# Loading the first batch through the casting DMA queue, in a fused cross-attention and maxout kernel

## The chip, the cores and the metric

The kernel runs on one core of one Trainium2 chip. A core has a matrix engine (TensorE, PE in the profile), a vector engine (VectorE, DVE), an activation engine (ScalarE, ACT), a general engine (GpSimd, POOL) and a synchronization engine (SyncE, SP). Each runs its own instruction stream in order and waits for the others by semaphores. SP and POOL also issue the DMA transfers here: SP's go by a hardware queue (q1 in the profile) and move bytes as they are; POOL's go by a software queue (q0) and can cast float32 to bfloat16 on the way. Matrix results land in PSUM, everything else lives in SBUF.

The metric is the device time of one execution in microseconds. The kernel before took 166.1 us, the median of five runs from 165.62 to 167.12.

## The reference

There are 8 batches with 8 heads each. For each head there is x (512 rows of 64) and a state (32 rows of 64).

```
scores = x @ state.T / 8          # 512 x 32
a      = softmax(scores)          # over the 32 states
xread  = a @ state                # 512 x 64
a2     = softmax(state @ x.T / 8) # over the 512 rows of x
sread  = a2 @ x                   # 32 x 64
rows   = concat(xread, sread)     # per batch 544 rows of 8 * 64 = 512
h      = max(rows @ w1, rows @ w2, rows @ w3)   # 768 wide
out    = h @ w_out                # 4352 x 512
```

Inputs and output are float32. The kernel computes in bfloat16 with float32 sums.

## The kernel before, in words

**Layout.** Batch b's x lies in `x_sb[b]`: partition p holds 4 consecutive rows of each of the 8 heads, so 8 runs of 256 numbers, and behind them 64 columns of ones (L82), which the state read (`sread`, L217) uses to get the denominator of its softmax from the same matmul. The states of two batches are loaded together (`st_f[k]`, `load_st`, L57), cast to bfloat16 twice side by side (`states_cast`, L126), transposed by PE and spread into `bds[k]` (`states`, L132 and L135), a block-diagonal layout in which a pair of heads can be served by one matmul. The rest of `bds[k]` must be zero, hence the memsets of `bds` (L104, L105, L322).

**The work per batch.** `x_transpose` puts x on its side in two halves, even heads (g = 0) and odd heads (g = 1): eight PE transposes into PSUM and a copy out (L151, L154). `scores` multiplies with the states and takes the exponential on ACT (L172, L177). `softmax` sums and divides (L184 to L187). `a_transpose` turns the weights (L198, L199). Instead of computing xread and multiplying it with W, `g_cols` (L240) multiplies the states with 384 columns of the three W at once (128 of each, a slice m of six) and ACT or DVE copies the result G out of PSUM (L246). `maxout` (L261) multiplies the transposed weights with G, three matmul pairs for the three W, and ACT (L265) and DVE (L268, L269) take the maximum. `ffn_out` (L286, L293) multiplies with w_out and stores by DMA (L297, L302).

**Weights.** W comes in three chunks of columns, of 1, 2 and 3 slices. Chunk 0, the first slice, is loaded as float32 by SP in three parts, one for each W (`w0_f`, L102), and cast by ACT (L332). Chunks 1 and 2 are loaded and cast by POOL's queue (`load_w`, L91), three transfers each.

**Order.** The order of all instructions is written out by hand: an engine executes its instructions in the order of the program text, and the tile framework adds only the semaphores. A PSUM or SBUF buffer of a rotating tag is taken when the one who had it is done: tag "pw" has four PSUM buffers, which the transposes, the maxout matmuls and the output matmuls take in turn; tag "two" has two larger ones. `keep_busy(n)` issues n matmuls on zeros whose result nobody reads (L117).

The first batch comes in like this. SP loads the first two batches' states, then x of batch 0 as float32 in two halves (`x0_f`, L75), then W's first slice in three parts. POOL builds the identity matrix, writes the ones of all eight batches and the zeros of `bds[1]`, and then issues the load of batch 1 and six loads of W. PE runs five filler matmuls, transposes the states, runs three more, and transposes batch 0 as DVE (even heads, L319) and ACT (odd heads, L320) have cast it. After the scores of batch 0 PE runs four fillers and goes on with the transposes of batch 1.

POOL's transfers take their completion semaphores from a group of eight in turn. A transfer that comes to a semaphore a second time is issued only when the earlier transfer on it has landed.

## Time and profile before

| | |
|---|---|
| five runs | 165.62, 166.04, 166.1, 166.91, 167.12 us |
| profiled execution | 166.1 us, of which the instructions span 164.3 us |
| busy share of the span | PE 93%, ACT 62%, DVE 58%, POOL 25% |
| 0 to 4 us | PE busy 2.81, ACT 1.49, DVE 1.18, POOL 3.40 us |
| 8 to 12 us | PE busy 3.64, ACT 2.23, DVE 2.56, POOL 1.34 us |
| 32 to 36 us | PE busy 3.59, ACT 2.78, DVE 3.62, POOL 0 us |
| bytes moved by DMA | 21.59 MB; 14.42 by POOL's queue, 6.95 by SP's |

The profile is of one execution. A group of instructions is named by the line of the kernel, the engine, and what it writes and reads. In the timeline and in the chain, the first number is the start in us and the second the duration; "x8" counts instructions; what stands in brackets is how long the engine was idle before the group and who released it. "PEld" is PE's loading of the stationary operand, which runs beside its matmuls.

### The profile page before, as it was taken

The numbers are of one execution on the slowest core, as the hardware profiler recorded it, in microseconds if no ns is written. First come the engines' busy times: TensorE is split into PE (matmuls) and PEld (weight loads), VectorE is DVE, ScalarE is ACT, GpSimd is POOL, SyncE is SP. The second block draws the span as 40 slices with busy tenths as digits, with TensorE's granted clock in tenths as the row PEclk, the third lists the DMA queues.
The fourth block names the chain that finished last, engine by engine and source line by source line (L and its number), as shares of the span: only waits on it lengthen the run. The fifth ranks groups of instructions, "written<-read, shape, count | busy, mean of one in ns | idle before, by whom it ended". The sixth has DMA issues, their size and how long they took to land.

```text
span 164.3 us, 3574 instructions
## 1 busy us (share of the span) xinstructions
PE 152.4 (93%) x1432; PEld 72.7 (44%) x1448; DVE 94.7 (58%) x160; ACT 101.7 (62%) x163; POOL 41.8 (25%) x61
## 2 busy tenths in 40 slices
PE   7699799998999999999999999999999999999990
PEld 2356243543345444444344444343444456665440
DVE  2573987879518653674548454855485555585001
ACT  3568458676896778854786688648764853333440
POOL 8933640105150601081016101410141010100140
PEclk9999999999999999999999999999999999999999
DMA  4999999900029999449991988460306030030374
GB/s 119 326 204 198 204 199 250 135 6 2 0 107 152 128 255 195 92 81 138 277 217 73 129 190 104 165 192 14 128 0 192 14 128 0 0 132 0 128 221 162
DMA packets 31824, 21.59 MB, mean 131 GB/s; under 512 B 15648, under 2 KB 29344, under 8 KB 31808
## 3 DMA queue, kind: packets, MB, share of 16 engines
q0 software_dynamic: 13520, 14.42, 42.4%
q1 hardware_dynamic: 18288, 6.95, 20.9%
q8 instruction: 11, 0.18, 0.4%
q14 instruction: 5, 0.04, 0.1%
HBM read 15.20 MB, written 8.91 MB: 147 GB/s over the span
## 4 chain that ended last, share of the span: by engine, by line
PE 63%; DVE 13%; ACT 12%; issue 4%; DMA 4%; POOL 1%; SPq 0%; DVEq 0%; ACTq 0%
PE pw L261 32%; PE po L286 20%; DVE t L268 4%; ACT G L246 4%; DVE ht L269 4%; PE pg L240 4%; DVE den L184 4%; DMA x0f<-in_x_dram 3%; ACT e L177 3%; ACT t L265 2%; PE ps L172 2%; PE psr L217 2%; DMA out_dram<-osb 1%; PE pxt L151 1%; PE idle L117 1%
## 5 line engine op out<-in xcount | busy, mean ns | idle before, releaser
L261 PE MATMUL pw<-aT,G 128*128 128x512 bf16 x288 | 71.3, 379 | 3.4 <-ACT G L246 2.1
L268 DVE TENSOR_TENSOR t<-t,pw 128x512 bf16<-128x512 bf16 (+1 forms) x54 | 35.0, 649 | 40.5 <-ACT t L265 38.5
L286 PE MATMUL po<-wout,ht 128*128 128x512 bf16 x188 | 47.9, 380 | 0.8
L261 PEld LDWEIGHTS <-G 128*128 128x128 bf16 x288 | 26.7, 98 | 36.1 <-issue 4.5
L246 ACT CAST G<-pg 128x768 bf16<-128x768 f32 x47 | 35.8, 805 | 8.3 <-PE pg L240 8.0
L265 ACT CAST t<-pw 128x512 bf16<-128x512 f32 (+1 forms) x54 | 30.5, 565 | 13.9 <-PE pw L261 12.4
L269 DVE TENSOR_TENSOR ht<-t,pw 128x512 bf16<-128x512 bf16 (+1 forms) x54 | 35.5, 658 | 5.6
L293 ACT COPY osb<-po 128x512 f32<-128x512 f32 x33 | 19.4, 587 | 21.2 <-PE po L286 20.7
L286 PEld LDWEIGHTS <-ht 128*128 128x128 bf16 x204 | 18.4, 98 | 23.6 <-issue 4.7
L302 POOL DMA_DIRECT2D out_dram<-osb x14 | 7.8, 559 | 70.2 <-ACT osb L293 70.2
L187 POOL TENSOR_TENSOR a<-e,rden 128x1024 bf16<-128x1024 bf16 (+1 forms) x8 | 14.4, 1800 | 36.4 <-DVE rden L186 29.8
L240 PE MATMUL pg<-w,bd 64*32 64x384 bf16 x384 | 13.2, 328 | 0.2 <-DVE G L246 0.2
L184 DVE TENSOR_REDUCE den<-e 128x32 f32<-128x1024 bf16 (+1 forms) x9 | 9.9, 1101 | 4.4 <-ACT e L177 4.4
L177 ACT ACTIVATE e<-ps 128x1024 bf16<-128x1024 f32 x7 | 7.2, 1025 | 4.6 <-PE ps L172 4.6
L261 PE MATMUL pw<-ats,w 128*128 128x256 bf16 x72 | 8.8, 273 | 0.0
L240 PEld LDWEIGHTS <-bd 64*32 64x32 bf16 x384 | 3.7, 89 | 11.0 <-issue 10.8
L261 PEld LDWEIGHTS <-w 128*128 128x128 bf16 x72 | 7.0, 98 | 2.1
L151 PE MATMUL pxt<-ident,x 128*128 128x128 bf16 x64 | 6.1, 260 | 1.8 <-ACT x L320 0.8
L135 ACT COPY bd<-pt 64x512 bf16<-64x512 bf16 x8 | 4.6, 580 | 4.1 <-PE pt L132 4.0
L151 PEld LDWEIGHTS <-x 128*128 128x128 bf16 x64 | 5.1, 119 | 4.1 <-DVE x L319 1.6
L117 PE MATMUL idle<-zero 128*128 128x512 bf16 x12 | 5.7, 630 | 1.2 <-DVE zero L78 1.2
L69 POOL DMA_DIRECT2D x<-in_x_dram x7 | 6.7, 956 | 0.0
(44 smaller groups left out, 67.1 us busy)
## 6 DMA issues: line engine op xcount, KB each, us to landing
out_dram<-osb POOLq DMA_DIRECT2D x14, 512.0 KB, 3.5
x<-in_x_dram POOLq DMA_DIRECT2D x7, 512.0 KB, 9.1
w<-in_moe_w_dram POOLq DMA_DIRECT2D x3, 384.0 KB, 13.6
x0f<-in_x_dram SPq DMA_DIRECT2D x2, 512.0 KB, 4.6
w0f<-in_moe_w_dram SPq DMA_DIRECT2D x3, 256.0 KB, 5.8
w<-in_moe_w_dram POOLq DMA_DIRECT2D x3, 256.0 KB, 10.0
wout<-in_moe_w_out_dram POOLq DMA_DIRECT2D x1, 768.0 KB, 16.1
out_dram<-osb SPq DMA_DIRECT2D x1, 512.0 KB, 2.7
```

Of the source, the lines that this page charges most:

```text
L151: nc.tensor.transpose(p[:, s, jj, :], xv[b][:, 2 * s + g, 2 * jj:2 * jj + 2, :].rearrange("p j d -> p (j d)"), ident)
L177: nc.scalar.activation(out=e[b][:, :, g0:g1], in_=p, func=AF.Exp, scale=scale)
L184: nc.vector.reduce_sum(out=den, in_=e[b][:, :, g0:g1], axis=AX.X)
L187: mul(out=a[b][:, :, g0:g1].rearrange("p j g s n -> p j (g s) n"), in0=e[b][:, :, g0:g1].rearrange("p j g s n -> p j (g s) n"), in1=rden.r ...
L240: nc.tensor.matmul(p[32 * s:32 * s + 32, g, 0:384].rearrange("p (i f) -> p i f", i=3), bd(b, 2 * s + g)[64 * g:64 * g + 64, g, :], w[64 * ...
L246: copy(out=G[b][:, :, m * 384:(m + 1) * 384], in_=p[:, :, 0:384])
L261: nc.tensor.matmul(p[:, 0:n], lhs(i, k), rhs(k), start=(k == 0), stop=(k == nk - 1))
L265: nc.scalar.copy(out=t0[:, 0:n], in_=pw[0][:, 0:n])
L268: nc.vector.tensor_max(t1[:, 0:n], t0[:, 0:n], pw[1][:, 0:n])
L269: nc.vector.tensor_max(ht[b][:, m, :], t1[:, 0:n], pw[2][:, 0:n])
L286: nc.tensor.matmul(p, ht[b][:, m, j * 128:(j + 1) * 128], wout_sb[:, m, :], start=(m == 0), stop=(m == NM - 1))
L293: nc.scalar.copy(out=o[:, j, :], in_=p)
```

## The change

Four things change in the prologue, and one copy later moves to another engine.

1. x of batch 0 is no longer loaded as float32 by SP and cast by DVE and ACT. POOL's queue loads and casts it, in two halves, as the first transfers that POOL issues.
2. W's first slice: parts 1 and 2 stay with SP and are cast by ACT; part 3 is loaded and cast by POOL's queue, behind x of batch 1.
3. The ones of all batches and the zeros of `bds[1]` are written by DVE, behind its cast of the first states, where it wrote `bds[2]` and `bds[3]`; these are no longer behind DVE's cast of x.
4. The second run of fillers has four matmuls instead of three.
5. The second pair of states is spread into `bds[1]` by DVE instead of ACT.

```diff
-    x0_f = [data.tile([128, HS, J * D], F32, name=f"x0f{g}") for g in range(2)]
-    for g in range(2):
-        nc.sync.dma_start(
-            out=x0_f[g], in_=x[0].rearrange("(s g) (p j) d -> g p s (j d)", g=2, j=J)[g])
     zero = const.tile([128, 512], BF16, name="zero")
     nc.vector.memset(zero, 0.0)
     ident = const.tile([128, 128], BF16, name="ident")
     make_identity(nc, ident)
-    for b in range(B):
-        nc.gpsimd.memset(x_sb[b][:, XW:XW + D], 1.0)
+    for g in range(2):
+        nc.gpsimd.dma_start(
+            out=x_sb[0][:, 0:XW].rearrange("p (s g jd) -> g p s jd", g=2, s=HS)[g],
+            in_=x[0].rearrange("(s g) (p j) d -> g p s (j d)", g=2, j=J)[g])
...
-    w0_f = wpool.tile([128, HS, 3, 128], F32, name="w0f")
-    for i, w in enumerate((moe_w1, moe_w2, moe_w3)):
+    w0_f = wpool.tile([128, HS, 2, 128], F32, name="w0f")
+    for i, w in enumerate((moe_w1, moe_w2)):
         nc.sync.dma_start(out=w0_f[:, :, i, :], in_=w.rearrange("(kk p) f -> p kk f", p=128)[:, :, 0:128])
     bds = [data.tile([128, 2, H, 2, Ns], BF16, name=f"bd{k}") for k in range(B // 2)]
     nc.vector.memset(bds[0], 0.0)
-    nc.gpsimd.memset(bds[1], 0.0)
     load_x(1)
+    nc.gpsimd.dma_start(out=w_sb[0][:, :, 2, :], in_=moe_w3.rearrange("(kk p) f -> p kk f", p=128)[:, :, 0:128])
     load_w(1)
     load_w(2)
...
     keep_busy(5)
     states_cast(0, dve)
     states(0, act)
-    keep_busy(3)
-    cast0 = xv[0].rearrange("p (s g) j d -> p g s (j d)", g=2)
-    dve(out=cast0[:, 0], in_=x0_f[0])
-    act(out=cast0[:, 1], in_=x0_f[1])
-    for k in range(2, B // 2):
+    for k in range(1, B // 2):
         nc.vector.memset(bds[k], 0.0)
+    for b in range(B):
+        nc.vector.memset(x_sb[b][:, XW:XW + D], 1.0)
+    keep_busy(4)
     x_transpose(0, 0, dve)
     x_transpose(0, 1, dve)
...
-    for i in range(3):
+    for i in range(2):
         act(out=w_sb[0][:, :, i, :], in_=w0_f[:, :, i, :])
...
     x_maxout(0, 4)
-    states(1, act)
+    states(1, dve)
     x_transpose(2, 0, dve)
     x_transpose(2, 1, dve)
```

## The prediction

> **What bounds the kernel now.** I first read the page's busy rows and the chain that ended last. TensorE (PE) is busy for 93% of the span, and from about 49 us the chain is almost all PE, with no wait on a load. No edit touches that part, so the change can only shift the moment at which it begins. Two stretches before it are touched: the first 15 us, and the 31 to 38 us stretch where the second pair of states is spread.

> ```profile
> PE 152.4 (93%) x1432; PEld 72.7 (44%) x1448; DVE 94.7 (58%) x160; ACT 101.7 (62%) x163; POOL 41.8 (25%) x61
> ...
> 1.66 5.12 DMA x0f<-in_x_dram
> 6.80 1.05 ACT x L320
> ...
> 7.90 1.05 PE pxt L151 x8
> ...
> 10.33 1.71 PE idle L117 x4
> 12.04 1.01 PE pxt L151 x8
> 13.07 1.01 ACT xT L154
> ```

> The chain in order of time: the second half of x of batch 0 lands at 6.80, ACT casts it until 7.85, PE transposes it at 7.90. After the scores PE runs four filler matmuls and then transposes batch 1. So x of batch 0 sets the start, but the fillers stand between it and batch 1. The timeline of the same stretch shows the queues, and one more wait:

> ```profile
> 1.20 0.96 SPq L75 DMA_DIRECT2D x0f<-in_x_dram  x2
> 2.20 1.63 SPq L102 DMA_DIRECT2D w0f<-in_moe_w_dram  x3
> 2.84 1.06 POOL L69 DMA_DIRECT2D x<-in_x_dram  x1
> 3.89 4.61 POOL L91 DMA_DIRECT2D w<-in_moe_w_dram  x6
> 6.03 1.04 PE L151 MATMUL pxt<-ident,x 128*128 128x128 bf16 x8 [0.74 <-DVE x L319]
> 11.99 1.54 PEld L151 LDWEIGHTS <-x 128*128 128x128 bf16 x16 [0.86 <-DMA x<-in_x_dram]
> ```

> Batch 1's x landed at 11.95; the fillers, 427 ns apart, would have let PE go at 11.83. So that load costs only 0.16 us today. The DMA view of single stretches shows who moves the bytes, first 7.0 to 7.5 us, then 8 to 9 us (packets, MB, share of the engines' time):

> ```profile
> q1 hardware_dynamic: 281, 0.14, 120.0%
> ...
> q0 software_dynamic: 187, 0.10, 69.6%
> q1 hardware_dynamic: 243, 0.12, 58.3%
> ```

> POOL's queue (q0) has not one packet before 7.5 us, 3.6 us after its first issue ended at 3.90; then it shares with SP's queue (q1).

> The second stretch, from the timeline:

> ```profile
> 32.23 1.18 ACT L135 COPY bd<-pt 64x512 bf16<-64x512 bf16 x2
> 32.47 0.69 DVE L269 TENSOR_TENSOR ht<-t,pw 128x512 bf16<-128x512 bf16 x1
> 33.07 1.28 DVE L154 COPY xT<-pxt 128x1024 bf16<-128x1024 bf16 x2
> 33.20 1.46 PE L261 MATMUL pw<-aT,G 128*128 128x512 bf16 x6 [0.18 <-DVE ht L269]
> 34.45 0.69 DVE L268 TENSOR_TENSOR t<-t,pw 128x512 bf16<-128x512 bf16 x1
> 35.90 1.02 ACT L177 ACTIVATE e<-ps 128x1024 bf16<-128x1024 f32 x1 [0.78 <-PE ps L172]
> ```

> DVE runs without a gap from 31.7 to 35.9. ACT has 0.43 us free at 33.4.

> [...] 8 transposes take 1.04 us at 6.03, and 16 take 1.08 us at 31.94. The starts of single transposes change spacing (107 to 56 ns) near 13.4 us. [...] DVE copies 128x512 bf16 from PSUM in 0.42 us.

> **The change, part by part.**

> *SP's queue.* Two 512 KB loads of x and one of three 256 KB loads of W go; SP issues W's two parts at 1.20 and 1.71 (0.51 each). SP's loads behind the state's had their first packets at about 3.1 us, 1.9 after the issue. The two parts are 2 x 512 packets; q1 alone moved 620 packets in the us from 6 to 7, so 1.65 us: done at about 4.75.

> *POOL's queue.* Eight memsets (0.76 us) and one of 0.95 us go. POOL issues x in halves from 1.25 instead of batch 1 at 2.84: 0.76 each by the L91 row (512 rows each), then batch 1 (1.06) at 2.78 to 3.84, W's third part 0.76, then the six of before, to 9.2 instead of 8.5. POOL next works at 11.16, so that is hidden by 2 us. POOL has eight semaphores in turn (109 to 116 in the trace; wout, the ninth issue, waited for the first's), so the ninth and tenth issues now wait for x's halves, at 7.7 and 8.5. Behind them stands only the product at 11.16.

> *When x starts on q0* is not in the trace; it is bounded so. Early: a store's first packet came 0.57 us after its issue ended when the queues were empty (issue ends 108.90, packets from 109.47); so 2.01 + 0.57 = 2.6 us, ahead of SP's. Late: 3.6 us after the issue, as the first POOL load did here, 5.7 us. Between: a store issued while SP had transposes in flight waited 2.1 us (100.96 to 103.1), until those were over; so behind SP's loads, 4.75 us. I take 4.75. q0 alone moved 390 packets a us of this size (367 from 10 to 11 with SP's rest beside it), so a half takes 1.31 us, and the semaphore came 0.35 us after the last data: halves at 6.4 and 7.7, batch 1 at 10.4, W's third part (half-size packets, estimate 0.9 us) at 11.3, then W's second slice at about 15.6 as against 15.98. Needed: 11.7, 14.1 and 17.3. Covered.

> *Casts.* DVE's 0.69 and ACT's 1.05 us cast of x go. PE starts the second half at 7.75 instead of 7.90, and the fillers end at 11.68: batch 1 starts 0.3 us earlier. As about the last third of its transposes ran at the fast rate before and would not now, 0.15 of that stays on the chain ACT xT, aT, G. ACT's third cast of W (0.62) goes too; ACT waited 0.56 us for PE there, so nothing.

> *DVE's memsets.* After the state's cast (3.35): three of 0.49, spaced 0.54, and eight of 64 columns, estimate 0.12 to 0.17 each from the zero row (0.27 for 256), so DVE is free at 6.0 to 6.3. Its next work is the copy of the first transposes, at 6.4 + 1.08 = 7.5. Hidden; with x at its earliest it would cost up to 0.8. The fourth filler ends at 5.5, before x: nothing.

> *states(1) from ACT to DVE.* Two copies of 64x512, 0.58 each on ACT. [...] 0.69 as DVE's 512-element reduce, spaced 0.60. DVE's queue, by hand: ht ends 33.15; copies 33.07 to 34.35; xT 34.27 to 34.95 and 34.87 to 35.55; t from 35.55 (34.45 before). PE's four small PSUM buffers turn: its second pair of matmuls needs the states' buffer (34.40 instead of 33.64), its third the first xT's (35.0 instead of 34.07); G's eight matmuls follow at 35.45, the scores at 35.75 instead of 35.17, the exp 0.56 us later. From there all hangs on the exp (t, G, the next pairs), so +0.55 goes to the end. ACT's saved 1.17 us gives nothing back: its next copy at 33.83 waited for PE. Bounds: [...] with nothing absorbed +1.2.

> Sum: -0.15 + 0.55 = +0.4 us. The profiled execution took 166.1 us (span 164.3 and 1.8 around it), which is also the median, so 166.5.

> **Rivals.** *x gets ahead of SP's loads (faster).* q0 starts at 2.6: halves at 4.3 and 5.6. PE is then busy from 1.19 to 7 us [...]; it needs batch 1 next, which shares with W's parts and lands at about 10.6, so its transposes start 1.3 us earlier and end 0.6 us sooner, of which W's second slice and the state loads (due at 29.4, cast until 30.2, used at 31.5) leave about 1.5. With +0.55: 165.1. For: in the trace SP's second load had no packet before 3 us. Against: q0's late start. It decides where x's second half lands before about 6.5.

> *The first POOL load is late for itself (slower).* 3.6 us after its issue whatever SP does: first packets at 5.7, halves at 7.35 and 8.65, 0.8 later than the cast data of before; batch 1's transposes start 0.65 late, of which 0.5 to 0.65 stays. With +0.55: 167.3. It decides from a second half landing past about 8.3. [...] For: the one first POOL load that the trace has. Against: SP's backlog explains it as well.

> *Only the move of states counts at less than I take:* [...] then 166.0 in the main case.

> **How the numbers follow.** Main case 0.38 (its range 165.8 to 167.2), x ahead 0.31, late 0.31. A measurement of this kernel, whose five runs lie 165.62 to 167.12, can tell about 0.5%, or 0.83 us. Main: 0.02 faster, 0.27 same, 0.09 slower; ahead: 0.26 faster, 0.05 same; late: 0.05 same, 0.26 slower. So 0.28, 0.37, 0.35. The range 164.9 to 167.8 leaves out the tails of both rivals.

> **What would show it.** The landing of x's second half (7.7), the start of PE's second eight transposes (7.75) and of batch 1's (11.7); DVE copies of bd near 33.1 with about 0.68 each; the exp of batch 2 shifted against the start of the stretch by 0.5. I am wrong if q0 has packets before 3 us, or none before 5.5; [...] or if the states' copies run at 0.42.

## The result, and the profile after

The changed kernel takes 167.62 us, the median of 31 runs (166.59 to 168.56), against 166.33 us for the kernel before, measured beside it (52 runs, 165.5 to 167.67). The ratio of the means (167.46 and 166.46 us) is 1.006, with a 95% interval of 1.0043 to 1.0077: slower by about 1.0 us. The profiled execution took 167.62 us with a span of 165.8 us, 1.5 us more than the span before.

The page's busy row, then the chain that ended last (start, duration, what), for the stretch shown of the kernel before:

```profile
PE 151.9 (92%) x1433; PEld 72.8 (44%) x1449; DVE 96.5 (58%) x170; ACT 99.3 (60%) x159; POOL 42.3 (26%) x55
```

```profile
2.37 6.16 DMA x<-in_x_dram
...
8.57 1.05 PE pxt L149 x8
...
11.00 1.71 PE idle L115 x4
12.71 1.71 PE pxt L149 x16
```

The second half of x lands at 8.53, where before it had landed at 6.78 and was cast at 7.85. Then the chain is the old one: scores, four fillers, batch 1, all later. The timeline of the changed kernel:

```profile
1.20 0.96 SPq L100 DMA_DIRECT2D w0f<-in_moe_w_dram  x2
1.46 1.69 POOL L78 DMA_DIRECT2D x<-in_x_dram  x2
...
6.89 0.62 PE L149 MATMUL pxt<-ident,x 128*128 128x128 bf16 x8 [1.90 <-DMA x<-in_x_dram]
8.57 1.03 PE L149 MATMUL pxt<-ident,x 128*128 128x128 bf16 x8 [1.06 <-DMA x<-in_x_dram]
...
12.50 1.91 PE L149 MATMUL pxt<-ident,x 128*128 128x128 bf16 x16
```

Two things are to be seen. PE stands idle 1.90 us and 1.06 us for x. And the first eight transposes take 0.62 us, the second 1.03: in between PE's clock went back to half (0.50 from 7.47 us on). Batch 1's transposes have no DMA wait any more: its x landed at 11.58, but the fillers held PE until 12.50. The windows view shows the clock (PEclk, third from the right; the columns ahead of it are the busy time of PE, PEld, DVE, ACT and POOL):

```profile
4.06:7.47 3.41, 1.51 (x13) 0.65 (x10) 1.49 (x10) 1.16 (x2) 3.41 (x5) 1.00 1.32 196
7.47:10.88 3.41, 1.99 (x26) 1.80 (x26) 1.56 (x3) 0.60 (x1) 1.77 (x3) 0.50 1.36 166
10.88:14.30 3.42, 3.42 (x24) 2.32 (x22) 2.44 (x5) 2.33 (x4) 2.47 (x3) 0.50 1.50 194
```

The record of the clock starts at its first change, which is the rise at 4.06 here. The kernel before has its first change at 13.38; the view shows 1.00 ahead of that, although single transposes started 107 ns apart up to there and 56 ns apart just behind it.

The DMA view of 4.3 to 5.0 us, where POOL's queue begins (packets, MB, share):

```profile
q0 software_dynamic: 152, 0.08, 86.0%
q1 hardware_dynamic: 145, 0.07, 32.9%
```

q0's first packet is at 4.34, and it meets the last of SP's W. The second stretch, in the timeline:

```profile
33.79 1.39 DVE L133 COPY bd<-pt 64x512 bf16<-64x512 bf16 x2
...
35.19 1.02 PE L259 MATMUL pw<-aT,G 128*128 128x512 bf16 x4 [0.67 <-ACT t L263]
35.21 1.29 DVE L152 COPY xT<-pxt 128x1024 bf16<-128x1024 bf16 x2
36.41 0.68 DVE L266 TENSOR_TENSOR t<-t,pw 128x512 bf16<-128x512 bf16 x1
37.17 1.02 ACT L175 ACTIVATE e<-ps 128x1024 bf16<-128x1024 f32 x1 [1.33 <-PE ps L170]
```

DVE's copies of the states end at 35.18, and PE's second pair, which needs their PSUM buffer, starts at 35.19. (The row names ACT, whose copy ended at 35.15, but PE's pair doesn't read or overwrite what that copy read.)

Set beside the kernel before, every exp (the exponential of a batch's scores) and every copy that ACT makes of a maxout result (t) or an output is about 0.71 us late from the exp of batch 1 on (15.92 against 15.20) and 1.28 us late from the exp of batch 2 on (37.17 against 35.90), and nothing more is lost until the last of them. The remaining 0.27 us of the span lies behind the last copy, at the program's end.

### The profile page after: what moved, and what is told of

Its sections match the earlier page's. It is cut to its first block, busy times and chain, and to the rows that moved or that the text cites. A ratio compares the mean times of both kernels' runs of the same rounds, so it can differ in the third digit from the quotient of the medians.

```text
span 165.8 us, 3571 instructions
## 1 busy us (share of the span) xinstructions
PE 151.9 (92%) x1433; PEld 72.8 (44%) x1449; DVE 96.5 (58%) x170; ACT 99.3 (60%) x159; POOL 42.3 (26%) x55
## 3 DMA queue, kind: packets, MB, share of 16 engines
q1 hardware_dynamic: 16704, 5.64, 17.3%
HBM read 15.20 MB, written 8.91 MB: 145 GB/s over the span
## 4 chain that ended last, share of the span: by engine, by line
PE 63%; DVE 13%; ACT 10%; DMA 5%; issue 5%; POOL 1%; DVEq 0%; ACTq 0%; POOLq 0%
PE pw L259 33%; PE po L284 20%; DVE t L266 4%; PE pg L238 4%; DVE ht L267 4%; DMA x<-in_x_dram 4%; DVE den L182 4%; ACT G L244 4%; ACT e L175 3%; ACT t L263 2%; PE ps L170 2%; PE psr L215 2%; PE pxt L149 2%; DMA out_dram<-osb 1%; PE idle L115 1%
## 5 line engine op out<-in xcount | busy, mean ns | idle before, releaser
L152 DVE COPY xT<-pxt 128x1024 bf16<-128x1024 bf16 x6 | 4.0, 688 | 4.4 <-PE pxt L149 4.4
L69 POOL DMA_DIRECT2D x<-in_x_dram x7 | 6.5, 933 | 0.0
## 6 DMA issues: line engine op xcount, KB each, us to landing
w<-in_moe_w_dram POOLq DMA_DIRECT2D x3, 384.0 KB, 13.4
wout<-in_moe_w_out_dram POOLq DMA_DIRECT2D x1, 768.0 KB, 15.6
```

## The experiments

The traces give four numbers for each kernel: when x's second half has landed at the last DMA engine, when PE starts on batch 1, and the exps of batch 1 and 2. Times are us of one execution each; the ratio to the kernel before, with its interval, comes from the timed runs.

| kernel | x, 2nd half | PE, batch 1 | exp 1 | exp 2 | exp 1 to 2 | ratio |
|---|---|---|---|---|---|---|
| before | 6.78 | 11.99 | 15.20 | 35.90 | 20.70 | 1 |
| changed | 8.53 | 12.50 | 15.92 | 37.17 | 21.25 | 1.006 (1.0043 to 1.0077) |
| e1 changed, states on ACT | 9.13 | 12.72 | 15.61 | 36.34 | 20.73 | 1.0012 (0.9988 to 1.0035) |
| e2 before, states on DVE | 6.97 | 12.64 | 16.53 | 37.78 | 21.25 | 1.0024 (1.0003 to 1.0045) |
| e3 changed, no W on SP | 7.03 | 10.93 | 15.46 | 37.80 | 22.34 | 1.0083 (1.0042 to 1.0123) |
| e4 changed, x ahead of identity | 9.35 | 13.32 | 16.78 | 38.02 | 21.24 | 1.0072 (1.0033 to 1.0112) |
| e5 e1 with W held back | 7.00 | 9.95 | 17.33 | 39.60 | 22.27 | 1.0273 (1.0235 to 1.0311) |
| e6 e5 with fillers | 7.74 | 11.37 | 18.65 | 40.28 | 21.63 | 1.0255 (1.0223 to 1.0286) |
| e7 before with fillers | 6.87 | 12.48 | 15.22 | 35.94 | 20.72 | 0.9971 (0.9957 to 0.9984) |
| e8 e7 with W held back | 6.52 | 10.59 | 22.22 | 44.20 | 21.98 | 1.0478 (1.0437 to 1.0519) |
| e9 e1 with fillers | 8.46 | 11.88 | 14.62 | 35.34 | 20.72 | 0.9934 (0.9912 to 0.9956) |
| e10 before, memsets on DVE | 6.74 | 11.79 | 17.17 | 38.86 | 21.69 | 1.0195 (1.0153 to 1.0238) |
| e11 before, one copy each | 6.64 | 11.86 | 14.60 | 35.87 | 21.27 | one execution |
| e12 changed with fillers | 8.35 | 11.41 | 14.15 | 35.42 | 21.27 | 0.9992 (0.9972 to 1.0012) |

A start can't be judged by one trace. The kernel before, e2 and e11 have the same instructions up to the states, and their exp 1 is at 15.20, 16.53 and 14.60. What decides is the ratio, and for the states the time from exp 1 to exp 2.

**The states' copies (e1, e2, e11).** e1 undoes this edit alone in the changed kernel, e2 makes it alone in the kernel before, and e11 gives each engine one copy.

```diff
-    states(1, dve)
+    states(1, act)      # e1; e2 is the reverse, in the kernel before
```

> The changed kernel with the second states spread by ACT again. The two traces stand 0.71 us apart up to the states and 1.28 us from the exp of batch 2 on. Theory (the states' copies on DVE cost 0.57 us, by PE's small PSUM buffers): the exp of batch 2 comes 0.71 us later than before, not 1.28, and the median falls by 0.5 to 0.6 us against the changed kernel, so about 1.0025 of before. Rival (the stretch is late for another reason, as the state load that landed later): it stays at 1.006 and the exp stays 1.28 late.

> The kernel before with only this edit: the second states spread by DVE. Theory: 0.57 us more (1.0034 of before), nothing different before 33 us, the exp of batch 2 at 36.5 instead of 35.9. Rival (ACT's freed 1.17 us gives it back): 1.000.

From the exp of batch 1 to that of batch 2 it is 20.70 and 20.73 us with the copies on ACT, 21.25 and 21.25 with DVE, whatever the start was: 0.52 to 0.55 us. The theory holds, and ACT's freed 1.17 us gives nothing back. The ratios agree in sign, with wide intervals: e1 is 1.0012 where the changed kernel is 1.006, e2 is 1.0024 where the kernel before is 1. By e1, the prologue alone costs 0.2 us, with an interval from -0.2 to +0.6; e2's exp of batch 2 is at 37.78 rather than 36.5 because its batch 1's x landed at 12.60 and PE was at half rate until 15.54 in that execution.

```diff
-    def states(k, copy):
+    def states(k, copy, copy2=None):
...
-            copy(out=bds[k][r, :, :, c, :].rearrange("p b h (q t) -> p (b h) q t", t=4),
+            (copy2 if copy2 and c else copy)(out=bds[k][r, :, :, c, :].rearrange("p b h (q t) -> p (b h) q t", t=4),
...
-    states(1, act)
+    states(1, dve, act)
```

> The kernel before with one of the two copies of the second states on DVE and the other on ACT. By the hand replay (DVE's queue and PE's four small PSUM buffers): PE's scores start 0.05 to 0.1 us later, so from the exp of batch 1 to that of batch 2 it is 20.75 to 20.8 us, against 20.70 before and 21.25 with both on DVE. Rival (the cost is DVE's time itself, 0.6 us per copy, less nothing): about half of 0.55, 20.98.

Neither: 21.27, as much as with both on DVE. The timeline of e11 shows what both theories left out:

```profile
33.20 0.58 ACT L135 COPY bd<-pt 64x512 bf16<-64x512 bf16 x1 [1.44 <-DVE bd L135]
...
33.83 1.02 PE L261 MATMUL pw<-aT,G 128*128 128x512 bf16 x4 [0.61 <-ACT bd L135]
```

ACT's copy waited 1.44 us for DVE's of the same tile, so the two ran one after the other: PE got the buffer at 33.78 all the same, and ACT's own queue was late as well. So e11 doesn't tell DVE's time from the buffer's; what it adds is PE's wait for that buffer, which this row names outright.

**The start of POOL's queue (e3, e4).** e3 takes W's first slice from SP; e4 moves POOL's two issues ahead of the identity matrix.

```diff
-    for i, w in enumerate((moe_w1, moe_w2)):
-        nc.sync.dma_start(out=w0_f[:, :, i, :], in_=w.rearrange("(kk p) f -> p kk f", p=128)[:, :, 0:128])
...
-    nc.gpsimd.dma_start(out=w_sb[0][:, :, 2, :], in_=moe_w3.rearrange("(kk p) f -> p kk f", p=128)[:, :, 0:128])
+    load_w(0)           # e3: all three parts, behind x of batch 1
...
-    for i in range(2):
-        act(out=w_sb[0][:, :, i, :], in_=w0_f[:, :, i, :])
```

> The changed kernel with W's first slice wholly on POOL's queue, behind x of batch 1; SP loads only the first states, and ACT casts none of W. Theory A (POOL's first transfer waits for SP's loads in flight): q0's first packet near 3.0 us instead of 4.34, the halves of x landed near 4.6 to 5 and 6 to 6.5 instead of 6.84 and 8.53. Theory B (the first software transfer takes about 2 us from the end of its issue whatever SP does): first packet again at 4.3, halves at about 6.3 and 7.9, for the shared packets alone. Both: the slowest DMA engine may still be up to 0.9 us behind the median one. The time can be lost again at W's second slice, which is 0.9 us further back in the queue.

> The changed kernel with POOL issuing both halves of x ahead of building the identity matrix, so about 0.7 us earlier. Theory A (it waits for SP's loads): first packet stays near 4.3 and the second half lands at 8.2 to 8.5; time unchanged. Theory B (fixed time from the issue): first packet near 3.6, the halves 0.5 to 0.7 earlier, time 0.3 to 0.6 us less. The identity is then ready near 3.1, before the states' transposes need it.

e3 lies between the two theories. Its first packet came at 3.09, but only 33 packets went from 3.0 to 4.0:

```profile
q0 software_dynamic: 33, 0.02, 66.7%
```

The stream began just before 4.0, and in the changed kernel it begins at 4.34. So SP's loads cost 0.4 us of start (theory A), and the first software load took about 1.6 us from the end of its issue (2.37) before it flowed, with no load of SP's in flight (nearer to theory B). The halves landed at 5.71 and 7.03 instead of 6.84 and 8.53. Of these 1.50 us, 0.70 are in the median DMA engine (6.94 against 7.64), and the rest is the slowest of the 16 DMA engines, which was 0.89 us behind the median in the changed kernel and 0.09 in e3. That this second part comes from SP's loads isn't shown: in e6 below, where SP moved no packet from 2.8 to 10.0 us, the slowest was 0.83 behind. In e4 the first packet came 0.63 us earlier (3.71), as theory B has it, but the median engine was done no sooner (7.75), the slowest at 9.35, and the time is no less (1.0072): by an estimate from the first packets and from the changed kernel's last packets of W (near 5.0 us), x started earlier only shares longer with W, about 1.3 us instead of 0.7. The time of e3 is not x's: its first slice of W landed at 13.07, and PE, waiting for it, fell to half rate from 15.7 to 19.1.

**Holding W back (e5, e6, e8).** In these, DVE writes one column of W's target before SP may load it. This is e5, beside the states on ACT:

```diff
-    for i, w in enumerate((moe_w1, moe_w2)):
-        nc.sync.dma_start(out=w0_f[:, :, i, :], in_=w.rearrange("(kk p) f -> p kk f", p=128)[:, :, 0:128])
...
+    nc.vector.memset(w0_f[:, 0, :, 0:1], 0.0)
+    for i, w in enumerate((moe_w1, moe_w2)):
+        nc.sync.dma_start(out=w0_f[:, :, i, :], in_=w.rearrange("(kk p) f -> p kk f", p=128)[:, :, 0:128])
     keep_busy(4)
```

> The changed kernel with the second states spread by ACT, and SP's two W loads held back: DVE writes one column of their target behind its memsets, so SP issues them near 5.7 us instead of 1.2. Theory (x of batch 0 is late because it shares the DMA engines with W at the start): the halves land near 5.7 and 7.0 as without W on SP, PE's second eight transposes start near 7.1 against 8.6 to 9.2, the exp of batch 1 comes 0.5 to 1 us earlier than in the version with states on ACT alone (15.6), and the time is 0.4 to 0.9 us below that version's. Rival (start of the software queue alone): second half again past 8, no gain. Risk: x of batch 1 now shares with W and lands near 11.

> As the run with W held back, with one filler matmul between the two halves' transposes and six instead of four before batch 1's. In six traces so far PE went to full rate after a window of 3.4 us with at least 78% busy (71% was not enough) and back to half after one with at most 33% (41% was not). Theory: no return to half rate before batch 1, so its transposes take 0.9 instead of 1.7 us, and 0.4 to 0.8 us less than the run with W held back alone. Rival (PE's rate is hidden there by the loads): same time.

> The kernel before with those fillers and SP's three W loads held back behind DVE's cast of x (issued near 6.0 instead of 2.2). Theory (POOL's first load waits for SP's loads in flight): q0's first packet near 6.5 instead of 7.56 or earlier, x of batch 1 lands 1.5 to 2.5 us before 11.95; but W's first slice lands near 11.5 and ACT's three casts of it then hold its copies back, so little or nothing of it reaches the end: 0.994 to 1.000. Rival (the first software load is slow by itself): first packet and landing as before.

x landed as the theory said in e5 (5.68 and 7.00, PE at 7.05, batch 1 already at 9.95), and the time was a miss by far: 2.7% slower. Two rows of e5's timeline:

```profile
5.64 0.94 SPq L319 DMA_DIRECT2D w0f<-in_moe_w_dram  x2
```

```profile
14.67 0.62 ACT L330 CAST w<-w0f 128x512 bf16<-128x512 f32 x1 [1.76 <-DMA w0f<-in_moe_w_dram]
15.20 1.01 ACT L150 COPY xT<-pxt 128x1024 bf16<-128x1024 bf16 x1
```

Now SP's queue is the one that comes late. Issued at 5.64, its stream begins near 9.5, and from 11 to 12 us it moved 215 packets beside POOL's 218. W's second part landed at 14.65, and ACT's casts of it stand ahead of the copies of batch 1 in ACT's queue. e6 and e8 lose in the same place. In e6 the rate held until 17.80, so batch 1's transposes took 1.07 us as its theory had it, but the time stayed that of e5, as its rival had it. In e8 the three casts started at 14.05, 16.55 and 19.56, and 1.0478 is far outside the 0.994 to 1.000 expected. e8's rival falls as well: q0's first packet came at 5.72 instead of 7.56 and batch 1's x landed at 10.07.

**The memsets (e10).** e10 moves only the memsets of the kernel before, so that POOL issues batch 1 at 1.46.

```diff
-    for b in range(B):
-        nc.gpsimd.memset(x_sb[b][:, XW:XW + D], 1.0)
-    nc.gpsimd.memset(bds[1], 0.0)
...
+    for k in range(1, B // 2):
+        nc.vector.memset(bds[k], 0.0)
+    for b in range(B):
+        nc.vector.memset(x_sb[b][:, XW:XW + D], 1.0)
     keep_busy(3)
...
-    for k in range(2, B // 2):
-        nc.vector.memset(bds[k], 0.0)
```

> The kernel before with only the memsets moved: ones and the zeros of the second states on DVE behind the first states' cast, so POOL issues batch 1 near 1.46 instead of 2.84, SP's loads unchanged. Theory (the queue that is first at the engines goes on, the other waits and then shares): q0's first packet near 3.2 instead of 7.56, x's halves shared with batch 1, the second half landing past 8 instead of 6.78, 1.003 to 1.010 of before. Rival (SP's loads keep ahead): first packet past 6, x lands as before, 1.000.

1.0195, and by neither path. x landed as before (5.21 and 6.74). The stream of batch 1 began near 6 us, in front of SP's loads of W. In ACT's timeline:

```profile
12.17 0.62 ACT L331 CAST w<-w0f 128x512 bf16<-128x512 f32 x1 [0.74 <-DMA w0f<-in_moe_w_dram]
14.58 0.62 ACT L331 CAST w<-w0f 128x512 bf16<-128x512 f32 x1 [1.79 <-DMA w0f<-in_moe_w_dram]
```

W's parts landed at 9.67, 12.14 and 14.56 instead of 7.68, 8.59 and 10.70. In the kernel before, the 1.7 us of memsets on POOL had kept batch 1's load behind most of W. In the changed kernel W's two parts landed at 4.54 and 5.36, long before ACT casts them at 11.53, so there the move does not delay them.

**PE's rate (e7, e9, e12).** These add fillers: five or six instead of three or four ahead of x, two between x's halves, and six instead of four ahead of batch 1. This is e9, which has the states on ACT too:

```diff
-    keep_busy(4)
+    keep_busy(6)
     x_transpose(0, 0, dve)
+    keep_busy(2)
     x_transpose(0, 1, dve)
...
-    keep_busy(4)
+    keep_busy(6)
     x_transpose(1, 0, act)
...
-    states(1, dve)
+    states(1, act)
```

> The kernel before with more fillers: five instead of three ahead of x, two between its halves, six instead of four ahead of batch 1. Theory: PE reaches full rate by about 8 us [...] and stays there: batch 1's transposes (which start when its x lands, near 12) take 0.9 instead of 1.7 us, of which 0.4 to 0.5 us is on the path: 0.997 of before. Rival (hidden by ACT's copies and DVE): 1.000.

> The changed kernel with the second states on ACT and PE kept at full rate by fillers, as far as the kernel before was in the run with more fillers (six ahead of x, two between its halves, six ahead of batch 1); so x by POOL against x by SP with PE's rate taken out. Theory (the second half of x lands 0.7 to 1.5 us later than ACT's cast gave it before): the exp of batch 1 at 15.4 to 15.9 against 15.22, 0.998 to 1.002 of before, that is 0.2 to 0.7 us above the 0.9971 of before with fillers. Rival (the loss of the start was only PE's rate): 0.997 here too.

> The changed kernel with only the fillers added (six ahead of x, two between its halves, six ahead of batch 1); the second states stay on DVE. Theory (two separate costs: PE's rate at the start, and 0.55 us for the states' copies on DVE): 0.9934 + 0.0033 = 0.997 of before, 0.5 us above the version with ACT; from the exp of batch 1 to that of batch 2 21.25 to 21.3 us against 20.72. Rival (with the start earlier the states' copies are no longer on the path): 0.993.

e7 is 0.9971, as expected. Its trace doesn't show the gain: the exp of batch 1 is at 15.22 against 15.20, as batch 1's x landed at 12.44 against 11.95 in that execution. Only the timed runs do.

e9 is 0.9934: faster than both kernels, and beyond its own rival. The theory that x by POOL costs 0.2 to 0.7 us falls. In e9's timeline x's second half is as late as in the changed kernel, and still batch 1 is early:

```profile
7.05 0.62 PE L149 MATMUL pxt<-ident,x 128*128 128x128 bf16 x8 [1.06 <-DMA x<-in_x_dram]
...
8.50 0.62 PE L149 MATMUL pxt<-ident,x 128*128 128x128 bf16 x8 [0.40 <-DMA x<-in_x_dram]
...
10.15 1.46 PE L115 MATMUL idle<-zero 128*128 128x512 bf16 x6
11.88 1.07 PE L149 MATMUL pxt<-ident,x 128*128 128x128 bf16 x16 [0.27 <-DMA x<-in_x_dram]
```

At full rate the second half's transposes take 0.62 us instead of 1.03, six fillers 1.46 where four had taken 1.90, and batch 1's 1.07 instead of 1.91. PE waits for batch 1's x again, and that landed at 11.84, 0.6 us before e7's 12.44. The exp of batch 1 is at 14.62 against e7's 15.22. So with PE's rate held, the changed prologue as a whole (x by POOL, W's third part, the memsets, one filler more) is ahead of the old one by 0.6 us in these executions and by 0.0037 in the ratio; the two intervals (0.9912 to 0.9956 and 0.9957 to 0.9984) do not overlap.

e12 is the changed kernel without most of its loss at the start: 0.9992, with the states' 0.55 us still there (21.27). That is above the 0.997 expected. Between it and e9 the ratios differ by 0.0058, 0.96 us; the traces account for 0.55 of that, and the rest is within the intervals.

The clock recorded with the timed runs agrees. Of the changed kernel's executions, the ten with a mean clock of 0.975 to 0.977, as in the trace above, took 167.62 to 168.56 us; the eleven with 0.983 to 0.990 took 166.59 to 167.26. (The other eleven, at 0.993 and more, took 167.38 to 167.94; as the record starts at the first change, it leaves out a late first rise, as the one at 13.38 in the trace of before.) Three of e12's 22 runs show 0.987 or 0.988 and took 167.12 to 167.27 us, where the others took at most 166.67: it seems that even these fillers do not hold the rate in every execution.

## Why the prediction was right, and where it was wrong

The forecast of 166.5 us in a range of 164.9 to 167.8 had the right sign and less than half of the size: +0.4 us against +1.0 by the ratio, +1.5 in the profiled pair. Of its two terms the one for the states was right, and the credit of 0.15 us for the start was not. That the sum still fell into the range is in part luck: the range had been drawn wide enough for both rivals.

*states(1) from ACT to DVE.* Right, +0.55 forecast and 0.57 measured between the two traces (1.28 less 0.71). The steps of the replay hold too: copies of 0.68 and 0.70 us (0.69 assumed), the end of the second one at 1.39 us from the start, PE's pair stalled until it ended. (These copies of 64x512 read PSUM with step 128; DVE's copies of 128x512 that read it without a step took 0.41 to 0.42 us in the kernel before. That the step makes the difference was not shown: no run varied it by itself.)

*SP's queue and POOL's queue.* The issues were about where they were put: POOL at 1.46 to 3.15 (1.25 to 2.78 forecast), POOL's last W load at 8.81 after a wait of 0.32 us for x's second half, which the forecast had named and rightly taken as hidden. W's slices came in time.

*When x starts on q0.* The start of 4.75 was nearly right (4.34); the landing of 7.7 was not (8.53). The step that failed is the transfer: 1.31 us a half and 0.35 to the semaphore, 2.97 in all, took 4.19. SP's last 145 packets were shared with (at 390 packets a us, 0.37), and the slowest DMA engine was 0.89 behind the median; with 2.97 this makes 4.23. The forecast had read the late start of q0 in the trace of before as a wait behind SP's loads. e3 says that in the changed kernel about 1.6 of the 2.0 us from the end of the issue are the first software load itself, so 4.75 came near 4.34 for a reason that was only partly right.

*Casts.* "PE starts the second half at 7.75" is 8.57, so the credit of 0.15 became a debt: 0.71 us between the two traces, though in the timed runs of e1 only about 0.2, with 0 inside the interval. The forecast let batch 1 start with the fillers' end, and that was the right limit: 12.50, with its x there at 11.58. But it counted the fillers at half rate as given. e7, e9 and e12 show what that rate is worth: the fillers alone take the changed kernel from 1.006 to 0.9992, and with the states on ACT from 1.0012 to 0.9934, but the kernel before only from 1 to 0.9971. The trace shows how x's later arrival leaves PE idle longer: from 4.06 to 7.47 it streamed matmuls for a third of the time (1.51 us in the windows view, which counts each matmul to its modelled end; without that tail 33%), after which its clock was halved until 14.30. The forecast's sum had nothing of this. And of batch 1's transposes in the trace of before not the last third ran at the fast rate: only the last two of sixteen started sooner than 107 ns after the one ahead. All sixteen took 1.71 us there and 1.91 in the changed kernel.

*DVE's memsets and the third cast of W.* Hidden, as forecast: DVE was free at 5.61, before its copy at 7.54.

*The rivals.* The faster one did not come: q0 began after 4 us and not ahead of SP. The slower one did not come by its mechanism (first packet at 5.7), but past its point, a second half later than 8.3; and the 1.6 us of e3 are a part of its mechanism, a first software load that is late by itself.

What stays open is why the slowest DMA engines land x's second half up to 1.6 us behind the median one. The slowest was 0.89 behind in the changed kernel, 1.30 in e1, 1.60 in e4, 0.53 in e9 and 0.71 in e12, but 0.09 in e3 and 0.07 in e5. An overlap of the two queues does not explain it alone: in e6, where SP moved nothing from 2.8 to 10.0 us, it was 0.83. No run varied it by itself. Nor was DVE's time told from the PSUM buffer's hold in the states' copies.

## What to carry to other kernels

Price a transfer that opens a kernel by its last engine and with what shares the queues, not by its first packet; and ask of every load put earlier what it now stands in front of, since the loads of W that came second lost two to four microseconds in e10. PE's clock went from 1.00 to 0.50 here behind 3.41 us in which it streamed for 33%, so a longer wait can cost twice, once as idle time and once as the slower rate of what follows: a few matmuls that nobody reads, put into the gap, were worth 0.3% in one kernel and 0.7% in the other. And small PSUM buffers in rotation make the engine that empties them part of the matmul's path: a copy moved to a busy engine can hold up PE (0.57 us here), even when it saves another engine's time (1.17 us).

## What the runs showed of the hardware

**Two DMA queues.** In e5 SP's loads, issued at 5.64 while POOL's queue moved 372 to 383 packets a us (7 to 9 us), had a stream from about 9.5, where those issued at 1.20 in the kernel before had it from 3.1. Once both queues flowed there, they had about equal numbers of packets (218 of POOL's and 215 of SP's from 11 to 12 us).

**Two copies out of one tile.** Put on DVE and ACT in e11, they ran one after the other (ACT waited 1.44 us for DVE's), and from the exp of batch 1 to that of batch 2 it took 21.27 us, as with both on DVE (21.25).
